# Tiles 2 and 3 of the first block turned in a bank of `psK` instead of `psT`, and another order table for VectorE, ScalarE and the transfers

## The chip, the cores and the metric

The kernel runs on one core of one Trainium2 chip. The metric is the device time of one execution in microseconds (us). Three runs of the kernel before took 1146.65, 1143.88 and 1146.52 us (median 1146.52); one further execution was taken with the hardware profiler.

A core has five engines with queues of their own: TensorE (PE; its weight loads are shown apart as PEld), VectorE (DVE), ScalarE (ACT), GpSimd (POOL) and SyncE (SP), which here issues nearly all transfers. Each runs its instructions in the order in which they were laid down; between engines, semaphores make one wait for another. TensorE writes only to the eight PSUM banks, from which VectorE and ScalarE read.

## The reference, cut to what matters

```python
x = A_x                                    # 2048 x 576
mod = silu(c) @ w_mod                      # six vectors sa, ca, ga, sb, cb, gb
h = layernorm(x) * (1 + ca) + sa
q, k, v = split(h @ wqkv)                  # 32 heads of 18
pq, pk = phi(q), phi(k)                    # phi(t) = where(t > 0, t + 1, exp(t)) + 1e-6
kv, z = sum over s of pk (x) v, sum over s of pk
x = x + ga * ((pq @ kv) / (pq @ z + 1e-6)) @ wo
h = layernorm(x) * (1 + cb) + sb
x = x + gb * (silu(h @ w1) @ w2)           # 576 -> 4608 -> 576
```

## The kernel before

**Stages.** The 2048 tokens are 16 tiles of 128, t = 0 to 15, in four blocks of 512. Every matrix product is done in three passes, with a high and a low half of each factor (`A.copy` makes the high half, `sub_hi` or `w_lo` subtracts it from the full value to get the low one). The first stage, to about 204 us, projects k and v of each tile, sums kv, and projects q of the first half of the tiles. A short stage then builds the product of kv with wo. The second stage, from about 217 us, does the attention of all tiles and the first units of the MLP; the third, from about 370 us to the end, is the MLP alone. TensorE's order is the order of the code throughout.

**The order of the other engines in the first stage.** VectorE, ScalarE, GpSimd and SyncE run the first stage in an order that is written out by hand: the table `FIRST`. `arrange(FIRST, begun)` numbers the instructions of one engine as they stand in the code, and ties each to the one before it in the table. The ties are no waits: they only lay down the queue. So an instruction that the table puts ahead of another is issued first, and whatever stands behind it on that engine waits while it waits.

**The first block.** Its four tiles are read as rows, normalised, and turned: `turn_tiles` lets TensorE transpose 128x128 pieces into PSUM (L452), five per tile, and `modulate` and `split_h` read a piece of two tiles (128x256) from PSUM into `raw`, scale and shift it, and write the high and the low half into `hT` (L213 or L215, L219, L135). Tiles 0 and 1 come first; tiles 2 and 3 are `turn_half`, called behind v(0). Blocks 1 to 3 are turned another way: VectorE transposes 32x32 pieces (L298), a transfer writes them to memory (`turned`, L301) and others read them back (`acc<-turned` L306, `h<-turned` L308); ScalarE and VectorE then modulate and split them (`turn`).

**k, v and q.** k(0) and k(1) are made in passes as the chunks of weights come (L471). Each k and q then goes through phi: ScalarE takes exp from PSUM (e, L373), VectorE takes max(t, 0) + 1e-6 from PSUM (L378) and adds min(e, 1) (L382). A k is split into `pk` (L394 on ScalarE, L135 on VectorE). v goes from PSUM into `vx` in three pieces, each a high half on ScalarE (L643) and a low half on VectorE (L135). v's weights are split by L358 on ScalarE and L363/L365 on VectorE; q's (`wq`) by L358 on ScalarE and L363/L365 on GpSimd. `kv_mm` sums kv (L657). TensorE's order after k(0) and k(1) is: v(0), turn of tiles 2 and 3, v(1), kv of tile 0, q(0), q(1), k(2), v(2), kv, q(2), k(3), and so on.

**PSUM.** The first stage holds three banks for kv (`kvp`; kvp[1] and kvp[2] also serve the turning), one bank `psT`, and two buffers `psK` of two banks each, taken in turn by every `ps2()`: the first turning, k(0), k(1), v(1), q(0), q(1), k(2) and so on, to the five products with wo at L805 (j = 0 to 4). v(0) uses `psT` and kvp[0]. A tile can be written when the tile that had the buffer before has been read out. The second stage has three buffers `big` of two banks and two banks `small` in the same eight banks; the second `big` tile, the one of the first q in this stage, lies in the banks of the first `psK` buffer, and the two `small` ones lie in those of the second.

Of the kernel before, what the change touches and what calls it, by code (L numbers as in the profile page):

```python
# [22 lines left out]
def kernel(ctx: ExitStack, tc, A_x, A_wqkv, A_wo, B_x, B_w1, B_w2, c, w_mod, out):  # L23
# [32 lines left out]
    def behind(instructions):  # L56

        with ExitStack() as order:
# [36 lines left out]

    FIRST = {
        "DVE": """
            2 1 0 4-5 3 6-7 9-10 8 11-13 15 14 16-23 26 24-25 28 27 29-38 43-44 46-47 40 45 48-49 39 41 51 42 50
            53-54 52 55 60 56 61-62 57-58 88-90 63-69 71-72 70 73-75 77-78 76 79-80 91 59 81-87 93 92 94-96 152 97
            99-101 103-104 106-107 98 110-112 102 105 109 113-114 108 127-128 130-131 116 129 132-134 136-137 135  # L100
            138-139 115 119-121 140-146 122 117 123 118 153 124-125 154 147-149 126 155 150-151 156-159 161-162 160
            163-164 193-194 196-197 195 198 165 199-200 202-203 201 204-205 167 171 168 206-211 172-174 212 166 175
            169 176 170 177-184 190-192 185 213-215 186 216-217 219 218 223 220 224 221-222 187 234 238 188 231-232
            189 235-237 233 240-251 225 252-254 230 255-257 239 258-259 226 260 227 261-263 228-229
        """,
        "Activation": """
            0-4 6-7 5 8-10 13 11-12 14-19 21 20 22-25 27-28 26 29 31 30 32 41-43 36 39 33 37 40 48 50 52 38 34 44-47
            49 56 51 57 53 58 35 59 54-55 60-62 65-67 70 73 63 68 64 77 71 78 69 79 75 72 80 76 81-82 74 83 85-87
            91-92 88 84 89-90 93-99 104 101 100 102 107 103 105 111 108 112 106 116-117 109 126-127 113-115 110
            118-125 128-130 133 138 134 131 140 132 139 144 135 141 136 149 137 145 150 142-143 146-148 151-170  # L110
        """,
        "Pool": """
            0-1 3-4 2 6-7 5 8-12 15-17 13-14 18-20
        """,
        "SP": """
            0-30 32-33 31 62 34-38 40-41 39 42-45 48-49 47 46 63-65 50-53 66 54 56-57 55 70-73 58-61 67-68 78-79
            84-88 90-91 89 92-95 80-82 69 74-77 83 96 99 98 100-102 97 106 103-105
        """,
    }

# [100 lines left out]
    def modulate_split(*chunk):  # L221

        modulate(*chunk, A)
        return split_h(*chunk)
# [43 lines left out]
    def psT():  # L268
        t = psA.tile([P, 512], F32, name="psT")
        return t  # L270

    def ps2():
        t = psA.tile([P, 2, 512], F32, name="psK", bufs=2)
        return t
# [174 lines left out]
    def turn_tiles(pT, tiles, chunks):  # L449
        for i in tiles:  # L450
            for k in chunks:
                T.transpose(pT[k][:, i % 2 * P : i % 2 * P + P], x0s[i][:, k * P : (k + 1) * P], ident)  # L452

    def half_args(u, k, pT):
        return pT[k], k, hT[0][:, :, u * 256 : u * 256 + 256], cols["a"], h32[5 * u + k]

    def rooms(t):
        return dict(enumerate((t[:, 0:256], t[:, 256:512], kvp[1][:, 0, :], kvp[1][:, 1, :], kvp[2][:, 0, :])))

    def turn_half():  # L460

        pT = rooms(psT())
        turn_tiles(pT, (2, 3), START)
        for k in START:
            modulate_split(*half_args(1, k, pT))
# [10 lines left out]
    if True:  # L476
# [22 lines left out]
        pT = rooms(ps2()[:, 0, :])  # L499
# [180 lines left out]
    if True:  # L680
        for t in range(NT):
# [18 lines left out]
            if t == 0:  # L700
                for k in START:
                    split_w(wqp_, k, acc[10 + k], G)
                turn_half()
                xx = load_block(1)
# [29 lines left out]
    with tc.manual_schedule(engines={mybir.EngineType.PE}):  # L734
# [57 lines left out]
        rooms = [wg.tile([P, 4 * D], F32, name="w") for _ in range(NP0)]  # L792
# [197 lines left out]
    rooms, rooms0, fp, ts = [], {}, None, None  # L990
# [626 lines left out]
```

## Time and profile before

| | us |
|---|---|
| three runs | 1146.65, 1143.88, 1146.52 |
| the profiled execution, in all | 1145.4 |
| its span, first to last instruction | 1143.7 |
| TensorE busy in the span | 1123.4 |
| VectorE, ScalarE, GpSimd busy | 985.5, 527.2, 658.8 |

The profile is one execution. A page gives busy times and the chain of work that ended last; other views of the same trace give the waits, the groups of instructions, a timeline, and busy times by stretch. Times are in us from the start of the span. A timeline row has the start, the time taken, the engine, the line of the code, the operation, out<-in by the program's names, the shapes, and in brackets the idle time of the engine before it with what ended it. Rows of several instructions (x4) run from the first's start to the last's end; neighbours overlap a little, since an engine begins the next instruction before the last one has left it. "L243" is a line of the code; a helper has one line for all its callers, so the names of the tiles tell more.

The views that matter are shown with the prediction.

### The profile page before, as it was taken

How to read it: one execution, taken by the hardware profiler on the slowest of the kernel's cores; microseconds unless marked ns; L12 is line 12 of the kernel's file. 1: busy time of each engine (PE TensorE's matmuls, PEld its weight loads, DVE VectorE, ACT ScalarE, POOL GpSimd, SP SyncE). 2: the span in 40 equal slices, each digit the busy share in tenths (PEclk: the TensorE clock that was granted, in tenths of full speed). 3: DMA queues.
4: the chain of work that ended last, by engine and by line, in shares of the span. 5: the costliest groups of instructions: out<-in, count | busy, mean ns of one | idle time of the engine just before them, and what ended most of it. 6: DMA issues, size and time to landing. Idle time of an engine off the chain costs nothing.

```text
span 1143.7 us, 19402 instructions
## 1 busy us (share of the span) xinstructions
PE 1123.4 (98%) x7071; PEld 1037.0 (91%) x7071; DVE 985.5 (86%) x1557; ACT 527.2 (46%) x1078; POOL 658.8 (58%) x748
## 2 busy tenths in 40 slices
PE   6999999999999999999999999999999999999998
PEld 4899999899998899999999999999999999999998
DVE  5868765687988999999999999999999999999996
ACT  4644342447455544444445444444454444444441
POOL 3300000454714777767775776677667757776786
PEclk9999999999999999999999999999999999999999
DMA  9367963123458977976968869769779787697684
GB/s 289 81 174 163 168 80 63 56 72 125 151 197 296 369 274 257 343 275 255 362 257 312 312 248 351 273 248 365 263 274 335 263 334 286 253 345 273 250 310 155
DMA packets 103022, 279.03 MB, mean 244 GB/s; under 512 B 40652, under 2 KB 63440, under 8 KB 79888
## 3 DMA queue, kind: packets, MB, share of 16 engines
q1 hardware_dynamic: 102756, 277.50, 70.2%
q8 instruction: 56, 0.92, 0.3%
q10 hardware_dynamic: 172, 0.30, 0.1%
q14 instruction: 38, 0.31, 0.1%
HBM read 256.27 MB, written 21.51 MB: 243 GB/s over the span
## 4 chain that ended last, share of the span: by engine, by line
PE 94%; DMA 3%; DVE 2%; ACT 1%; issue 0%; SPq 0%; DVEq 0%; ACTq 0%
PE up L1348 34%; PE down L1421 32%; PE psK L243 12%; PE big L243 7%; PE small L911 2%; PE big L922 2%; PE kvp L657 2%; DMA acc<-in_A_wqkv_dram 1%; DMA hT<-in_w_mod_dram 1%; PE psK L805 1%; PE big L837 1%; DMA room<-hd 1%; PE small L228 1%; PE up L1451 1%; PE down L1451 1%; DVE st L190 0%
## 5 line engine op out<-in xcount | busy, mean ns | idle before, releaser
L1429 DVE TENSOR_TENSOR acc<-down,acc 128x576 f32<-128x576 f32 x330 | 246.1, 753 | 13.9 <-PE down L1421 4.1
L1348 PE MATMUL up<-hT,w 128*128 128x512 f32 x916 | 240.3, 391 | 0.0
L1348 PEld LDWEIGHTS up<-hT,w 128*128 128x128 f32 x916 | 164.5, 188 | 25.7
L1383 POOL TENSOR_TENSOR s<-f,f 128x256 f32<-128x256 f32 x66 | 51.9, 786 | 163.7 <-ACT f L1364 163.7
L1421 PE MATMUL down<-w,hc 128*128 128x288 f32 x792 | 120.7, 295 | 0.0
L1421 PE MATMUL down<-w,hb 128*128 128x288 f32 x792 | 120.7, 294 | 0.0
L1421 PEld LDWEIGHTS down<-w,hb 128*128 128x128 f32 x792 | 113.6, 188 | 5.9 <-DVE U L1429 0.3
L1421 PEld LDWEIGHTS down<-w,hc 128*128 128x128 f32 x792 | 113.6, 188 | 5.6
L1429 DVE TENSOR_TENSOR U<-down,U 128x576 f32<-128x576 f32 x132 | 99.4, 753 | 18.0 <-PE down L1421 15.7
L135 DVE TENSOR_TENSOR w<-v,w 128x288 fp32r<-128x288 f32 (+1 forms) x170 | 111.6, 666 | 0.1
L243 PE MATMUL psK<-w,hT 128*128 128x256 f32 (+1 forms) x638 | 102.4, 297 | 1.0 <-DVE acc L378 1.0
L1348 PE MATMUL up<-room,w 128*128 128x512 f32 x348 | 93.2, 396 | 1.1 <-DMA room<-hd 1.1
L243 PEld LDWEIGHTS psK<-w,hT 128*128 128x128 f32 x638 | 91.6, 189 | 1.3 <-DVE acc L378 1.3
L1402 POOL TENSOR_TENSOR hc<-s,hc 128x512 fp32r<-128x512 f32 x66 | 89.6, 1358 | 0.0
L1364 ACT ACTIVATE f<-f 128x512 f32<-128x512 f32 x102 | 64.4, 631 | 47.8 <-DVE f L1369 25.4
L1367 DVE TENSOR_TENSOR f<-up,p 128x512 f32<-128x512 f32 x102 | 69.7, 683 | 14.8 <-PE up L1348 10.1
L1348 PEld LDWEIGHTS up<-room,w 128*128 128x128 f32 x348 | 62.4, 188 | 12.4 <-DVE f L1369 1.5
L1091 ACT CAST w<-v 128x288 fp32r<-128x288 f32 x85 | 36.6, 434 | 76.8 <-PE down L1421 54.8
L1387 POOL TENSOR_TENSOR f<-f,s 128x256 f32<-128x256 f32 x66 | 50.9, 771 | 34.3 <-DVE hb L1402 28.7
L196 POOL TENSOR_TENSOR rstd<-ve,neghalf 128x4 f32<-128x4 f32 (+3 forms) x10 | 9.9, 995 | 102.2 <-DVE ve L195 101.2
L1421 PE MATMUL down<-w,hd 128*128 128x288 f32 x396 | 63.3, 295 | 0.0
L1421 PE MATMUL down<-w,he 128*128 128x288 f32 x396 | 63.1, 295 | 0.0
(302 smaller groups left out, 2519.6 us busy)
## 6 DMA issues: line engine op xcount, KB each, us to landing
hT<-hd SPq DMA_DIRECT2D x66, 1280.0 KB, 5.7
hT<-hd SPq DMA_DIRECT2D x45, 1024.0 KB, 4.9
room<-hd SPq DMA_DIRECT2D x35, 1280.0 KB, 6.3
room<-hd SPq DMA_DIRECT2D x20, 1024.0 KB, 5.7
v<-in_B_w_dram SPq DMA_DIRECT2D x17, 576.0 KB, 6.6
v<-in_B_w_dram SPq DMA_DIRECT2D x17, 512.0 KB, 7.5
hd<-S SPq DMA_DIRECT2D x6, 1024.0 KB, 5.9
xt<-in_A_x_dram SPq DMA_DIRECT2D x16, 288.0 KB, 6.0
```

The lines of the kernel that those rows point to most:

```text
L135: return V.tensor_sub(lo, full, f32(hi))
L243: T.matmul(ps, xpart(a), wpart(b), start=n == 0, stop=n == len(XW) - 1)
L657: T.matmul(o, vt[:, j, h, :], pkt[:, :, j * HG : j * HG + P], start=(t == 0 and h == 0 and j % 2 == 0), stop=(t == NT - 1 and h == 1), ski ...
L1091: A.copy(self.w2[n][:, 0], src)
L1348: T.matmul(ps, left, right, start=first and m == 0, stop=m == len(seq) - 1, skip_group_check=True)
L1364: A.activation(self.f[i, k], self.f[i, k], AF.Silu)
L1367: V.tensor_add(f, self.bank[bank[1]], self.p1)
L1383: G.tensor_add(self.s[:, 0:1], half(i, 0, 1), half(i, 1, 1))
L1387: G.tensor_sub(half(i, 1, 0), half(i, 1, 0), self.s[:, 1:2])
L1402: eng.tensor_sub(t[:, :, 1, :], src, f32(t[:, :, 0, :]))
L1421: T.matmul(ps[:, p, :HALF], self.a[i, n][:, u, p * P : (p + 1) * P], self.w.w2[n][:, v], start=n in (1, 5, 7, 6) and j == 0, stop=j == 2, ...
L1429: V.tensor_add(dst, ps[:, :, :HALF], dst)
```

## The change

`turn_half` takes its first bank from `ps2()` instead of `psT()`: chunks 0 and 1 of tiles 2 and 3 are turned in the first bank of a `psK` buffer (the one that k(0) had), chunks 2 to 4 in kvp[1] and kvp[2] as before. One more `psK` tile is taken, so all later ones change their buffer with each other: v(1) takes k(1)'s instead of k(0)'s, and so on to L805.

The table `FIRST` is another one for VectorE, ScalarE and SyncE; GpSimd's is the same, and so are TensorE's order and the number and kind of all instructions. In the new order, among others:

- VectorE: the first four steps of the statistics of tiles 0 and 1 are taken tile by tile, and two of those of tile 2 earlier, among the modulations. max and add of k(0) (L378, L382) come before the last three low halves of v's weights instead of behind them; pk(0) and phi of k(1) come before all of vx(0). Of hT's five low halves of tiles 2 and 3, two stand between the pieces of vx(1), two behind them, and one behind max of q(0).
- ScalarE: one cast of a weight stands before hT's casts. pk(0) and e of k(1) come before the casts of wq; the five modulations come before the first piece of vx(1), and the five casts of hT among and behind its pieces. In blocks 1 to 3 the modulations and casts of hT stand otherwise among the casts of vx, pk and the e of k and q.
- SyncE: two of the four transfers `acc<-turned` of block 2 are issued behind the four loads of xt for block 3, in place of ahead of them; some loads of w_mod are issued later.

```diff
--- before.py
+++ after.py
@@ -95,26 +95,26 @@
 
     FIRST = {
         "DVE": """
-            2 1 0 4-5 3 6-7 9-10 8 11-13 15 14 16-23 26 24-25 28 27 29-38 43-44 46-47 40 45 48-49 39 41 51 42 50
-            53-54 52 55 60 56 61-62 57-58 88-90 63-69 71-72 70 73-75 77-78 76 79-80 91 59 81-87 93 92 94-96 152 97
-            99-101 103-104 106-107 98 110-112 102 105 109 113-114 108 127-128 130-131 116 129 132-134 136-137 135
-            138-139 115 119-121 140-146 122 117 123 118 153 124-125 154 147-149 126 155 150-151 156-159 161-162 160
-            163-164 193-194 196-197 195 198 165 199-200 202-203 201 204-205 167 171 168 206-211 172-174 212 166 175
-            169 176 170 177-184 190-192 185 213-215 186 216-217 219 218 223 220 224 221-222 187 234 238 188 231-232
-            189 235-237 233 240-251 225 252-254 230 255-257 239 258-259 226 260 227 261-263 228-229
+            2 1 0 4-5 3 6-13 15 14 16-23 26 24-25 28 27 29-32 43 33-36 44 37-38 46-47 40 45 48-49 39 41-42 51-52 55
+            50 53-54 56-58 61 60 62 88 63 89 64 90 65-66 68-69 71-72 70 73-75 77-78 76 79-80 91 67 59 81-87 93 92
+            94-96 152 97 99-101 103-104 106-108 98 110-112 102 105 109 113-114 127-128 116 130-131 129 132-134
+            136-137 135 138-139 119-121 115 140-146 122 117 123 118 124-125 153 126 154 147-149 155 150-151 156-159
+            161-162 193-194 163 196-197 195 198-200 202-203 201 204-205 160 165 206-212 168 164 167 171-174 166 175
+            169-170 176-184 190-191 185 192 213-215 219 223 216-217 224 234 218 238 220-222 186-188 231-232 189 233
+            235-237 240-251 225 252-254 230 255-257 239 258-259 226 260 227-228 261-263 229
         """,
         "Activation": """
-            0-4 6-7 5 8-10 13 11-12 14-19 21 20 22-25 27-28 26 29 31 30 32 41-43 36 39 33 37 40 48 50 52 38 34 44-47
-            49 56 51 57 53 58 35 59 54-55 60-62 65-67 70 73 63 68 64 77 71 78 69 79 75 72 80 76 81-82 74 83 85-87
-            91-92 88 84 89-90 93-99 104 101 100 102 107 103 105 111 108 112 106 116-117 109 126-127 113-115 110
-            118-125 128-130 133 138 134 131 140 132 139 144 135 141 136 149 137 145 150 142-143 146-148 151-170
+            0-4 6-7 5 8-10 13 11-12 14-17 21 18-20 22-25 27-28 26 29 31 30 32-34 41-43 39 37 36 48 38 40 50 52 44 46
+            56 45 57 47 49 51 58 53 35 59 54-55 60-62 65-67 70 73-74 63 68 64 77 71 78 69 79 75 72 80 76 81-83 85-87
+            91-92 88 84 89-90 93-98 101-102 99 103-104 100 107 105 111 108 106 116 126-127 112 117 109 113-115 110
+            118-125 128-129 133 130 138 134 140 139 144 141 131 149 145 132 150 135-137 142-143 146-148 151-170
         """,
         "Pool": """
             0-1 3-4 2 6-7 5 8-12 15-17 13-14 18-20
         """,
         "SP": """
-            0-30 32-33 31 62 34-38 40-41 39 42-45 48-49 47 46 63-65 50-53 66 54 56-57 55 70-73 58-61 67-68 78-79
-            84-88 90-91 89 92-95 80-82 69 74-77 83 96 99 98 100-102 97 106 103-105
+            0-30 32 31 33 62 34-38 41 39-40 42-45 47 46 49 48 63-65 50-53 66 54 57 70 72-73 71 55-56 58-61 67-68 78
+            84-87 79 88 91 89-90 92-95 80-81 69 74-77 82-83 96 98-102 97 106 103-105
         """,
     }
 
@@ -459,7 +459,7 @@
 
     def turn_half():
 
-        pT = rooms(psT())
+        pT = rooms(ps2()[:, 0, :])
         turn_tiles(pT, (2, 3), START)
         for k in START:
             modulate_split(*half_args(1, k, pT))
```

## The prediction

> **What bounds the kernel now.** I read the page first.
>
> ```profile
> span 1143.7 us, 19402 instructions
> PE 1123.4 (98%) x7071; PEld 1037.0 (91%) x7071; DVE 985.5 (86%) x1557; ACT 527.2 (46%) x1078; POOL 658.8 (58%) x748
> ...
> PE 94%; DMA 3%; DVE 2%; ACT 1%; issue 0%; SPq 0%; DVEq 0%; ACTq 0%
> ```
>
> TensorE is busy 1123.4 of 1143.7 us, and the chain that ended last is 94% TensorE. No matrix work is added or removed, so the change can only touch the 20.3 us in which TensorE is idle. The next view cuts the span into stretches (us, TensorE busy, weight loads, VectorE, ScalarE, GpSimd, granted clock, DMA share, GB/s) to show where those 20.3 us lie.
>
> ```profile
> 0.00:29.00 29.00, 17.59 (x81) 13.70 (x81) 17.02 (x49) 12.80 (x25) 9.91 (x17) 1.00 0.91 285
> 29.00:56.00 27.00, 25.01 (x186) 24.52 (x187) 23.25 (x48) 17.18 (x36) 10.09 (x7) 1.00 0.31 77
> 56.00:204.00 148.00, 148.00 (x1123) 147.78 (x1121) 100.80 (x177) 58.06 (x114) 4.98 (x7) 1.00 0.68 127
> 204.00:220.00 16.00, 14.65 (x78) 12.11 (x77) 9.60 (x15) 7.53 (x13) 7.82 (x8) 1.00 0.25 78
> 220.00:1143.00 923.00, 918.11 (x5610) 838.87 (x5608) 834.80 (x1271) 431.62 (x892) 626.01 (x710) 1.00 0.73 269
> ```
>
> 11.4 us lie before 29 us, where input transfers set the pace; 2.0 between 29 and 56; none from 56 to 204, although the table reorders that stretch too; 1.35 from 204 to 220; 4.9 in the 923 us after. Third, the waits of TensorE from 29 to 220 us (waiter, releaser, us, times, longest):
>
> ```profile
> PE psK L243 <- DVE acc L378: 1.0, 1, 1.0
> PE big L243 <- DVE v L365: 1.0, 1, 1.0
> PE psT L452 <- DVE vx L135: 0.9, 1, 0.9
> ```
>
> Three long waits, 1.04 + 0.98 + 0.93 = 2.95 of the 3.35 us that the two stretches lack: that is nearly all there is to win between 29 and 220 us. I then went to each in the timeline, which has the exact figures.
>
> ```profile
> 33.41 0.28 PE L243 MATMUL psT<-w,hT 128*128 128x256 f32 x1
> ...
> 35.58 0.44 PE L452 MATMUL psT<-ident,xt 128*128 128x128 f32 x2 [0.93 <-DVE vx L135]
> ...
> 41.71 7.63 PE L243 MATMUL psK<-wq,hT 128*128 128x288 f32 x56
> 49.18 0.48 PE L243 MATMUL psK<-w,hT 128*128 128x288 f32 x2
> ...
> 54.15 0.54 PE L243 MATMUL psK<-w,hT 128*128 128x256 f32 x2 [1.04 <-DVE acc L378]
> ...
> 217.29 0.71 PE L837 MATMUL big<-ident,w 128*128 128x128 f32 x5
> 218.98 3.20 PE L243 MATMUL big<-wq,hT 128*128 128x288 f32 x22 [0.98 <-DVE v L365]
> ```
>
> 35.58 is the turning of tiles 2 and 3, which waits until v(0) is read out of the same bank. 41.71 is q(0) and q(1), 49.18 is k(2), 54.15 is v(2), which waits until q(1) has left its bank. 218.98 is the first q with the later pool `big`.
>
> **The change, part by part.** VectorE, ScalarE and GpSimd around these places:
>
> ```profile
> 29.64 1.43 DVE L363 TENSOR_TENSOR w<-acc,w 128x576 fp32r<-128x576 f32 x2
> 30.99 0.75 DVE L363 TENSOR_TENSOR w<-acc,v 128x576 fp32r<-128x576 f32 x1
> 32.56 0.76 DVE L378 TENSOR_SCALAR a<-psK 128x576 f32<-128x576 f32 x1
> 33.35 1.84 DVE L382 SCALAR_TENSOR_TENSOR a<-e,a 128x576 f32<-128x576 f32 x1
> 35.12 0.41 DVE L135 TENSOR_TENSOR vx<-psT,vx 128x252 fp32r<-128x252 f32 x1
> ...
> 42.93 0.23 DVE L135 TENSOR_TENSOR vx<-psK,vx 128x72 fp32r<-128x72 f32 x1 [0.28 <-ACT vx L643]
> 43.08 1.75 DVE L135 TENSOR_TENSOR hT<-raw,hT 128x256 fp32r<-128x256 f32 x5
> ...
> 53.38 0.72 DVE L378 TENSOR_SCALAR acc<-psK 128x576 f32<-128x576 f32 x1
> ```
>
> ```profile
> 29.68 0.65 ACT L373 ACTIVATE e<-psK 128x576 f32<-128x576 f32 x1
> ...
> 32.40 1.81 ACT L358 CAST wq<-acc 128x576 fp32r<-128x576 f32 x3
> ...
> 35.38 0.67 ACT L394 CAST pk<-a 128x576 fp32r<-128x576 f32 x1
> ...
> 40.35 0.71 ACT L219 CAST hT<-raw 128x256 fp32r<-128x256 f32 x2
> ```
>
> ```profile
> 38.45 3.40 POOL L363 TENSOR_TENSOR wq<-acc,wq 128x576 fp32r<-128x576 f32 x2
> ```
>
> *The bank of the turned tiles.* The ten transposes stay as they are; four of them now write a `psK` bank, whose k(0) VectorE reads out long before. The 0.93 us wait at 35.58 goes. Its cover is the early read of k(0) (L378): if that came after about 34.6, the wait would be back.
>
> *phi of k(0) ahead of three splits of w.* VectorE now runs L378 and L382 before the last three low halves of v's weights (the second of 29.64, 30.99, and the half one of L365 behind it). L378 follows e (29.68 + 0.65 = 30.33, in the new order about 0.45 earlier, since one weight cast moved ahead): about 29.9. L382 starts 0.79 later and holds VectorE 1.77, so the splits start near 32.45 and, 0.67 apart (two take 1.43, one 0.76), end at 33.2, 33.9 and 34.55. v(0) wants them from 33.41 on, 0.27 apart, and starts about 0.3 earlier than now (VectorE's last split of hT moves up by 0.5, and the wait for it, 0.25 at 29.01, goes; the row stands with the last rival): it waits step by step, ends near 35.1 instead of 34.5, and then transposes at once. Gain and loss meet: v(1) starts 0 to 0.35 us earlier. I take 0.2, the middle; it turns out to be covered by the next step.
>
> *pk(0) and e of k(1) ahead of the casts of wq on ScalarE.* pk waits for L382 (ends 32.55), and pk and e take a slot of 0.57 and 0.55 (0.67 and 0.65 less the overlap of 0.1 that the three casts in 1.81 show): the casts of wq start near 33.7 instead of 32.40. GpSimd's five low halves hang on them and run without pause to 38.45 + 3.40 = 41.85; now to about 43.15. The last one is chunk 1, which q(0) needs from its fifth pass, eight issues of 0.133 (7.48 us for 56) after 41.71, so at 42.77. Today it is there 0.9 early; after the change TensorE gets to this pass at 43.15 + 0.05 (the delay seen at 54.15 behind 53.38 + 0.72) = 43.2, +0.43 us, whatever v(1) gained. The bounds are 0.1 (GpSimd catching up on the way) and 0.9 (the casts another 0.5 late); I keep 0.43.
>
> *hT's low halves among the vx.* Two of the five 0.35 us steps of the row at 43.08 go into the pauses ahead of vx (0.28 in the row above, larger ones before it), one goes behind q(0)'s L378 but still ahead of q(1)'s, and v(1)'s first vx comes some 0.5 earlier, because ScalarE's casts of hT no longer stand before it (two of them take 0.71). From 42.93 to 53.38 VectorE has no pause, so q(1)'s L378 comes 0.5 + 0.35 = 0.85 earlier: it ends at 53.25.
>
> *v(2), the first sum.* TensorE ends k(2) 28 issues of 0.134 behind 49.18, near 52.93, and 0.43 later in the new order: 53.36, just behind VectorE's 53.25 + 0.05. So v(2) starts at 53.36 instead of 54.15: -0.8 us. The bounds are -0.3 (q(0) waiting 0.9) and -0.85 (VectorE alone decides).
>
> *Parity of the banks.* `psK` has two buffers in turn. One tile more is taken in the first block, so from there on each `psK` tile lies in the other buffer. That matters once, at 218.98: this `big` tile reuses the banks of one of them, and today that is the last one used (j = 4 at L805); now it is the one before (j = 3).
>
> ```profile
> 217.19 0.76 DVE L363 TENSOR_TENSOR v<-psK,w 128x576 fp32r<-128x576 f32 x1 [1.19 <-ACT w L358]
> 218.16 0.76 DVE L365 TENSOR_TENSOR v<-psK,v 64x576 fp32r<-64x576 f32 x1 [0.21 <-ACT v L358]
> ```
>
> j = 3 is read out at 217.95, when TensorE is still at L837 until 218.00. The 0.98 us wait shrinks to at most 0.1: -0.9 us, bounds -0.75 and -0.98. The buffer of j = 4 goes to `small`, which the first q don't use.
>
> *All else in the table* (the order of work on the later blocks, and of transfers) lies where TensorE never waits now. I cost it at 0; its cover is the distance of a k, v or q from the release of its bank. Upper bound: see the first rival.
>
> Sum: -0.8 - 0.9 = **-1.7 us**, bounds 1.05 and 1.85 below. Behind 220 us everything hangs on TensorE and moves with it. The profiled execution took 1145.4 us in all, 1143.7 of it span, which gives 1143.7. The runs shown are 1143.88, 1146.52 and 1146.65; the middle of all four is 1145.95, and 1145.95 - 1.7 = **1144.25 us** is the forecast.
>
> **The rivals.**
>
> *Slower: the second block comes back late.* Sync's queue now puts two of the four transfers `acc<-turned` of the second block behind four loads of xt. The rows of 96 to 106 us (KB each, median us to landing), one later transfer, and ScalarE's first use:
>
> ```profile
> xt<-in_A_x_dram SPq DMA_DIRECT2D x4, 288.0 KB, 8.8
> acc<-turned SPq DMA_DIRECT2D x4, 256.0 KB, 7.0
> ```
>
> ```profile
> raw<-parts SPq DMA_DIRECT2D x1, 576.0 KB, 13.2
> ```
>
> ```profile
> 107.12 1.52 ACT L213 ACTIVATE acc<-acc,col_a 128x512 f32<-128x512 f32 x2
> ```
>
> Issued near 99.3, at 7.0 or 8.8 they land at 106.3 or 108.1; ScalarE wants them from about 106.5. With 13.2 they land at 112.5, and ScalarE stands 5.4 us with the readouts of q and k behind it. Two buffers of 3.7 us each, less a readout of 0.65 + 0.76, give TensorE about 2 us of grace: it stalls 3.4, net +1.7, **1147.65**. It decides from a landing of about 10 us on. For it: this stretch already has the fullest DMA engines. Against it: VectorE's use of that block for k(8), at 125 us, leaves many us, and 13.2 belongs to a transfer of far smaller pieces.
>
> *No gain: the lead is handed back.* The longest wait of TensorE behind 220 us is for a transfer:
>
> ```profile
> PE up L1348 <- DMA room<-hd: 1.1, 1, 1.1
> ```
>
> Were that transfer paced by the queue instead of by TensorE, the 1.7 would end there: **1145.95**. Against it: the DMA engines are 73% busy there, and what is stored is computed from TensorE's own results.
>
> *Faster: the new waits don't appear.* If GpSimd and the splits keep up, all three waits go in full: -2.95, **1143.0**. Against it: GpSimd's five steps have no pause to catch up in, and the splits stand behind 0.76 + 1.84 us of work by order.
>
> *The slow start lasts longer.* The profile grants the full clock in every stretch, yet the early matmuls are slower:
>
> ```profile
> 15.98 1.78 PE L471 MATMUL psK<-w,hT 128*128 128x288 f32 x6 [1.15 <-DVE raw L215]
> ...
> 29.01 1.86 PE L471 MATMUL psK<-w,hT 128*128 128x288 f32 x12 [0.25 <-DVE hT L135]
> ```
>
> Six there take 1.78 us, twelve of the same shape here 1.86: 0.24 against 0.13 each. If the 24 that follow 24.8 us ran like the first, they would add 24 x 0.11 = 2.6: **1146.85**. Against it: nothing before 22 us moves. The Trainium skill (TensorE: Matmul & The Clock Gate, Part 1: The HAM clock gate) says that the array runs at half rate until a free-running window of about 3.4 us has been busy, and that the point of change varies from run to run. The doubled spacing agrees with it, the granted clock of 1.00 does not; by that rule the time could lie up to half a window, an estimated 1.7 us, to either side with no change at all.
>
> **How the numbers follow.** The forecast has 0.58, the faster case 0.13, no gain 0.15, the late block 0.09, the slow start 0.05. 1144.25 is the likeliest case's. Its own bounds are 1144.1 to 1144.9; the three runs shown lie 2.8 us (0.24%) apart, so 0.3%, 3.4 us, is about what a measurement of this kernel can tell from no change. The range 1142.0 to 1147.2 takes in the faster case and no gain with that spread and leaves out most of the late block. Faster by over 0.3% (below 1142.5): nearly half of the faster case and a sixth of the forecast, 0.16. Slower by over 0.3%: the worse third of the late block and of the slow start, a tenth of no gain, and a little for what I don't see: 0.08. The rest, 0.76, is within 0.3%.
>
> **What would show it.** Right: no wait at the transposes of tiles 2 and 3; small waits of v(0) on L363 and L365; one of 0.3 to 0.9 us of q(0) on GpSimd; none at v(2); at the second `big` 0.1 or less; TensorE full from 56 to 204 us; the 923 us after 220 unchanged to 1 us. Wrong: any TensorE wait between 56 and 204, above all on ScalarE near 107 us; a wait at `big` as long as now; or a changed length of the stretch after 220.

## The result, and the profile after

| | before | after |
|---|---|---|
| median of 22 runs each, us | 1145.63 | 1143.63 |
| span from lowest to highest, us | 1143.88 to 1147.1 | 1142.26 to 1147.72 |
| profiled execution in all, its span, us | 1145.4, 1143.7 | 1142.27, 1140.6 |

The ratio of the runs is 0.9987 with a 95% interval of 0.9981 to 0.9993: 1.5 us faster, 0.8 to 2.2 (the medians lie 2.0 apart). That is within 0.3%, and the interval leaves out 1. The page of the kernel after (span; busy time of each engine; shares of the chain that ended last):

```profile
span 1140.6 us, 19406 instructions
PE 1122.1 (98%) x7071; PEld 1036.0 (91%) x7071; DVE 985.2 (86%) x1557; ACT 526.9 (46%) x1078; POOL 659.6 (58%) x748
...
PE 96%; DVE 2%; DMA 1%; ACT 0%; issue 0%; ACTq 0%; DVEq 0%; SPq 0%
```

The work is the same, and the chain is TensorE's still more. The same cut by stretch as before (us, busy time of TensorE, weight loads, VectorE, ScalarE, GpSimd, then granted clock, DMA share, GB/s):

```profile
0.00:29.00 29.00, 17.37 (x88) 13.93 (x89) 18.00 (x50) 13.81 (x27) 10.48 (x17) 1.00 0.95 285
29.00:56.00 27.00, 26.07 (x194) 25.34 (x193) 23.87 (x49) 16.70 (x35) 9.03 (x6) 1.00 0.36 90
56.00:204.00 148.00, 147.63 (x1114) 146.81 (x1113) 99.33 (x175) 59.04 (x117) 5.76 (x8) 1.00 0.67 125
204.00:220.00 16.00, 16.00 (x95) 14.01 (x94) 10.58 (x17) 5.69 (x10) 8.60 (x9) 1.00 0.26 79
```

Idle time between 29 and 56 us fell from 1.99 to 0.93, between 204 and 220 from 1.35 to nothing. The 0.37 us that 56 to 204 now lacks are an old wait at the first L805, which has moved from 204.72 to 202.87 and so into this stretch. The waits of TensorE from 29 to 220 us (waiter, releaser, us, times, longest), then the rows of its timeline at the places of the prediction:

```profile
PE psK L243 <- POOL wq L363: 0.5, 1, 0.5
PE psK L805 <- ACT acc L375: 0.4, 1, 0.4
PE psK L243 <- DVE acc L378: 0.3, 1, 0.3
```

```profile
29.70 0.28 PE L243 MATMUL psT<-w,hT 128*128 128x256 f32 x1
...
33.17 0.35 PE L243 MATMUL psT<-w,hT 128*128 128x256 f32 x1
...
33.79 0.38 PE L452 MATMUL psK<-ident,xt 128*128 128x128 f32 x2
...
34.80 0.52 PE L243 MATMUL psK<-w,hT 128*128 128x256 f32 x2
...
41.66 6.66 PE L243 MATMUL psK<-wq,hT 128*128 128x288 f32 x48 [0.50 <-POOL wq L363]
...
52.36 0.54 PE L243 MATMUL psK<-w,hT 128*128 128x256 f32 x2 [0.32 <-DVE acc L378]
...
215.44 0.71 PE L837 MATMUL big<-ident,w 128*128 128x128 f32 x5
216.16 4.00 PE L243 MATMUL big<-wq,hT 128*128 128x288 f32 x28
```

29.70 is the start of v(0), 33.17 the pass of v(0) that waits a little for a split, 33.79 the turning of tiles 2 and 3 with no wait, 34.80 v(1), 41.66 q(0) waiting for GpSimd, 52.36 v(2), 216.16 the second `big` tile with no wait.

The steps behind v(0) are told as differences from its start, since that start itself varies from one execution to the next (30.71 before, 29.70 here; more on this at the end). The same three steps, for every kernel of this study (us; each number is a start in that kernel's timeline of TensorE or the difference of two, "q of big" being the first q in a `big` tile; in three kernels, marked *, v(2) starts within a row of six passes, and its start is reckoned from the spacing):

| kernel | v(0) | v(2) - v(0) | q of big - v(2) | ratio to before, 95% |
|---|---|---|---|---|
| before | 30.71 | 23.44 | 164.83 | |
| after | 29.70 | 22.66 | 163.80 | 0.9987 (0.9981, 0.9993) |
| after, once more | 29.52 | 22.65 | 163.84 | 0.9986 (0.9977, 0.9994) |
| bank alone | 30.25 | 27.87 | 163.78 | 1.0038 (1.0026, 1.0051) |
| table alone | 30.02 | 26.30 | 164.75 | 1.0034 (1.0020, 1.0047) |
| parity back | 32.34 | 22.55 | 164.38 | 0.9993 (0.9984, 1.0002) |
| q in order | 30.03 | 22.83 | 163.83 | 0.9984 (0.9975, 0.9992) |
| both waits * | 31.44 | 21.38 | 164.36 | 0.9983 (0.9974, 0.9992) |
| phi late | 30.32 | 23.93 | 163.98 | 0.9990 (0.9981, 0.9999) |
| hT behind | 30.18 | 22.70 | 163.79 | 0.9985 (0.9976, 0.9994) |
| pk behind | 30.13 | 22.20 | 163.90 | 0.9977 (0.9967, 0.9986) |
| max between * | 31.82 | 21.37 | 165.02 | 0.9980 (0.9971, 0.9989) |
| pk behind, z moved | 30.05 | 22.25 | 164.18 | 0.9983 (0.9973, 0.9992) |
| max between, z moved * | 30.01 | 22.18 | 164.33 | 0.9985 (0.9977, 0.9994) |

The change took 0.78 us from the way v(0) to v(2) and 1.03 from v(2) to the first q in `big`: 1.81 us from v(0) on. The runs, at 1.5 (0.8 to 2.2), agree with it.

A part of v(0)'s earlier start is the change's too. Ahead of v(0) the last passes of k(0) and k(1) waited twice for VectorE in the kernel before (28.26 below, and 29.01 in the prediction), and no longer do; the second row is of the kernel after:

```profile
28.26 0.50 PE L471 MATMUL psK<-w,hT 128*128 128x288 f32 x2 [0.24 <-DVE w L365]
```

```profile
27.00 2.86 PE L471 MATMUL psK<-w,hT 128*128 128x288 f32 x20
```

From VectorE's first copy of `e` (L438, at 22.86 before and 22.28 after) to v(0) it is 7.85 us before and 7.86 with the bank alone. With the new table it is 7.40 to 7.42 in the nine profiles whose clock was not cut there. So the table takes 0.44 us ahead of v(0), and the steps of the profiles come to 2.25 us, a little above the interval of the runs.

### The profile page after: what moved, and what is told of

It is laid out like the page before. It is cut to its first block, busy times and chain, and to the rows that moved or that the text cites. A ratio compares the mean times of both kernels' runs of the same rounds, so it can differ in the third digit from the quotient of the medians.

```text
span 1140.6 us, 19406 instructions
## 1 busy us (share of the span) xinstructions
PE 1122.1 (98%) x7071; PEld 1036.0 (91%) x7071; DVE 985.2 (86%) x1557; ACT 526.9 (46%) x1078; POOL 659.6 (58%) x748
## 4 chain that ended last, share of the span: by engine, by line
PE 96%; DVE 2%; DMA 1%; ACT 0%; issue 0%; ACTq 0%; DVEq 0%; SPq 0%
PE up L1348 34%; PE down L1421 32%; PE psK L243 12%; PE big L243 7%; PE small L911 2%; PE big L922 2%; PE kvp L657 2%; PE psK L805 1%; PE big L837 1%; PE psK L471 1%; DMA room<-hd 1%; PE small L228 1%; PE up L1451 1%; PE down L1451 1%; DMA tmod<-in_w_mod_dram 1%; DVE hT L135 0%
## 5 line engine op out<-in xcount | busy, mean ns | idle before, releaser
L1348 PE MATMUL up<-hT,w 128*128 128x512 f32 x916 | 240.4, 391 | 0.0
L1348 PEld LDWEIGHTS up<-hT,w 128*128 128x128 f32 x916 | 164.5, 188 | 25.9
L1348 PE MATMUL up<-room,w 128*128 128x512 f32 x348 | 93.2, 396 | 1.1 <-DMA room<-hd 1.1
L1348 PEld LDWEIGHTS up<-room,w 128*128 128x128 f32 x348 | 62.4, 188 | 12.3 <-DVE f L1369 1.5
L196 POOL TENSOR_TENSOR rstd<-ve,neghalf 128x4 f32<-128x4 f32 (+3 forms) x10 | 9.8, 976 | 98.4 <-DVE ve L195 67.5
```

Of the source, the lines that this page charges most:

```text
L1348: T.matmul(ps, left, right, start=first and m == 0, stop=m == len(seq) - 1, skip_group_check=True)
```

## The experiments

**The changed kernel once more.**

> The changed kernel once more, for a second profile and a second timing. Theory (the gain is three waits between 29 and 220 us: 0.93 at the transposes of tiles 2 and 3, 1.04 at v(2) less what is left of it, 0.98 at the second big tile): the waits of TensorE from 29 to 220 us are again 0.5 on GpSimd, 0.3 at v(2) and none at big, and the time is 1.5 to 2 us below the kernel before. Rival (much of the 3.1 us between the two profiled spans is the early stretch, which comes out by chance): the start of v(0), 29.70 us in the changed kernel and 30.7 in the one before, comes anywhere between the two, and the span moves with it.

1143.13 us against 1144.98 for the kernel before, ratio 0.9986. The three waits are the same to 0.1 us, and so are both differences in the table. Yet the span of this execution is 1143.1, 2.5 us longer than that of the first. v(0) came earlier, not later: the rival is wrong about the place. The excess lies at one later wait:

```profile
377.12 1.93 PE L1348 MATMUL up<-room,w 128*128 128x512 f32 x6 [2.33 <-DMA room<-hd]
...
381.14 1.81 PE L1348 MATMUL up<-hT,w 128*128 128x512 f32 x6
...
378.00:382.00 4.00, 4.00 (x15) 3.42 (x14) 2.06 (x3) 1.49 (x3) 3.83 (x6) 0.57 0.68 234
```

The first two rows are its timeline, the third a stretch of 4 us there. The same rows in the first execution of this kernel:

```profile
375.98 1.65 PE L1348 MATMUL up<-room,w 128*128 128x512 f32 x6 [1.07 <-DMA room<-hd]
...
378.72 1.53 PE L1348 MATMUL up<-hT,w 128*128 128x512 f32 x6
```

TensorE waited 2.33 us for the transfer `room<-hd` instead of 1.07, and behind it TensorE was granted 0.57 of its clock over 4 us, which cost 1.3 us more: the lag behind the first execution is 377.12 - 375.98 = 1.14 at the wait and 381.14 - 378.72 = 2.42 a little on. A difference of a single pair of spans is therefore no measure of this change. Each run has its granted clock on record. In this batch the runs at 1.000 average 1142.75 us (7 of 11) against 1144.86 for the kernel before (18 of 21): 2.1 us, near the 2.25 of the steps. So cut clocks may be what brings the ratio down to 1.6 us, but this rests on few runs.

**Bank and table, each alone.**

The kernel before with the bank of the kernel after:

```diff
-        pT = rooms(psT())
+        pT = rooms(ps2()[:, 0, :])
```

The kernel after with the bank of the kernel before:

```diff
-        pT = rooms(ps2()[:, 0, :])
+        pT = rooms(psT())
```

> The bank of the turned tiles is changed, the order table is the old one. Theory (bank and table are one edit: v(1) now takes k(1)'s buffer, and the old table reads k(1) late, e at 38.28 and L378 at 38.99 + 0.76 us): the 0.93 us wait at the transposes goes and the 0.98 at big goes, but v(1) waits until about 39.8 us, some 3 us later than its 36.65; net 2 us slower than the kernel before, about 1147.7. Rival (the parts add up, each removes its own wait): 0.93 at the transposes is swallowed by v(2), 0.98 at big stays won, 1.0 us faster than before, about 1144.6.

> The new order table, but tiles 2 and 3 are turned in psT as before. Theory (bank and table are one edit): the transposes wait for the low half of vx out of psT, which the new table puts behind phi of k(1), at 35.98 + 0.40 us instead of 33.79: a wait of about 2.6 us, of which the 0.5 on GpSimd is given back; the 1.0 at big is there again; net 3 us slower than the changed kernel, about 1 to 1.5 us slower than the kernel before. Rival (the parts add up): the table's 0.8 us at v(2) is kept, and it is 0.8 to 1 us faster than the kernel before.

Both are slower than the kernel before, by 4.3 and 3.9 us by their ratios. So the parts don't add up; each needs the other. The rows of the bank alone, its timeline and then two stretches (the number before the last two is the granted clock):

```profile
39.36 0.51 PE L243 MATMUL psK<-w,hT 128*128 128x256 f32 x2 [4.12 <-DVE a L378]
39.70 0.43 PE L243 MATMUL psK<-v,hT 128*128 128x256 f32 x2
39.98 3.24 PE L243 MATMUL psK<-w,hT 128*128 128x256 f32 x14
...
40.00:42.00 2.00, 2.00 (x11) 2.00 (x11) 0.00 (x1) 0.52 (x2) 1.28 (x1) 0.60 1.06 227
42.00:44.00 2.00, 2.00 (x10) 2.00 (x10) 0.00 (x0) 0.00 (x0) 0.00 (x0) 0.55 0.63 226
```

v(1) now lies in k(1)'s buffer, and the old table reads k(1) late: a wait of 4.12 us at just the time expected. And of the table alone:

```profile
36.85 0.41 PE L452 MATMUL psT<-ident,xt 128*128 128x128 f32 x2 [2.56 <-DVE vx L135]
...
38.00:40.00 2.00, 2.00 (x10) 2.00 (x9) 0.23 (x1) 1.58 (x4) 1.92 (x2) 0.50 0.21 30
```

The wait for the low half of vx, 2.56 us, is the 2.6 that theory named. What no theory named is the rest: behind both waits TensorE ran at half its clock for about 3.4 us, which costs an estimated 1.7 us, half of that. The fourteen passes of v(1) that take 2.05 us in the kernel after took 3.24 with the bank alone. That is most of the 2.3 us (bank alone) and 2.4 to 2.9 us (table alone) by which they came out slower than expected. The table of differences also shows the two edits apart where they don't meet: with the new bank the way from v(2) to `big` is 163.8, with the old one 164.8, whatever the table.

**The parity of the banks, undone in the changed kernel.**

```diff
-        psz = ps2()
+        psz = psT(), kvp[0].rearrange("p a b -> p (a b)")
...
-        A.copy(halves(z), psz[:, :, :HALF])
+        for h in range(2):
+            A.copy(z[:, h * HALF : (h + 1) * HALF], psz[h][:, :HALF])
```

(ScalarE's later table is numbered anew for the second copy.)

> The changed kernel, with the product for z in psT and kvp[0] instead of a psK tile, read out in two copies: one psK tile less, so the last five tiles change buffers again. Theory (the second big tile waits for whichever product with wo had its banks last): the wait of about 1.0 us at big is back; the 0.37 us wait at the first L805 goes, since this tile no longer has the buffer of the q just ahead; net +0.6 us on the changed kernel. Rival (the wait at big went because VectorE is earlier there, not because of the bank): big doesn't wait, net -0.4 us on the changed kernel.

The ratio is 0.9993 against 0.9986 for the changed kernel in the same batch, +0.8 us where +0.6 was expected (the intervals overlap; the profile is what decides here). Its timeline, whose line numbers are 5 lower:

```profile
205.11 2.10 PE L801 MATMUL psK<-raw,tmod 126*128 126x288 f32 x8
...
217.58 0.71 PE L833 MATMUL big<-ident,w 128*128 128x128 f32 x5
219.27 0.93 PE L238 MATMUL big<-wq,hT 128*128 128x288 f32 x5 [0.98 <-DVE v L360]
```

The wait at `big` is back with its old length, on the same split of the last product, and the 0.37 us wait at the first product (205.11) is gone. VectorE's order is that of the changed kernel, so the bank is the cause. As the programs are built, the second `big` tile lies in PSUM banks 4 and 5 before, after and here; the last product (j = 4) lies in 4 and 5 before and here, and in 6 and 7 in the changed kernel.

**q's weights in the order of use.** The changed kernel casts and splits chunks 2, 3, 4 of `wq` before 0 and 1. Here it goes 0 to 4 (the casts on ScalarE, the low halves on GpSimd).

```diff
-            ... 32-34 41-43 39 37 36 48 38 40 50 52 ...
+            ... 32-34 39-42 37 36 48 38 43 50 52 ...
-            0-1 3-4 2 6-7 5 8-12 15-17 13-14 18-20
+            0-1 3-4 2 6-7 5 8-20
```

> The changed kernel with the weights of q cast and split in the order in which q(0) uses them (chunks 0 and 1 first in place of last). Theory (the waits of q(0) and v(2) are in series: TensorE's and VectorE's ways to v(2) are 0.32 us apart): the 0.50 us wait on GpSimd goes, v(2) waits 0.8 instead of 0.3, the time stays that of the changed kernel to 0.2 us. Rival (a wait that is removed is won): 0.5 us faster than the changed kernel.

Ratio 0.9984 beside 0.9986 and 0.9987, and the wait moved on, as expected:

```profile
40.19 7.63 PE L243 MATMUL psK<-wq,hT 128*128 128x288 f32 x56
...
52.86 0.53 PE L243 MATMUL psK<-w,hT 128*128 128x256 f32 x2 [1.31 <-DVE acc L378]
```

q(0) and q(1) run through; v(2) waits 1.31 instead of 0.32, more than the 0.8 expected, and starts 22.83 us behind v(0), no earlier than without the edit. VectorE's max of q(1) is what v(2) stands on.

**Both waits taken away.**

```diff
-            ... 91 67 59 81-87 93 92 94-96 ...
+            ... 91 67 59 81-85 93 86-87 92 94-96 ...
```

(q's weights are in the order of use here too.)

> As the one before, and on VectorE max of q(1) stands behind two of block 1's four transposes instead of all four, 1.37 us earlier. Theory (in series): now both waits go, 0.5 + 0.3 = 0.8 us faster than the changed kernel, about 2.3 to 2.8 below the kernel before, and TensorE has no wait from 34 to 202 us. Rival (two transposes come 0.7 us later, block 1 comes back later and another wait takes the place): a new wait between 56 and 204 us, no gain.

v(2) comes 1.28 us earlier against v(0) than in the changed kernel, without a wait; but on the way to `big` 0.56 is given back, and the ratio, 0.9983, can't be told from the changed kernel's. The rows, of TensorE (at 52.19 four passes of k(2) and the first two of v(2) stand in one row) and of ScalarE:

```profile
52.19 1.18 PE L243 MATMUL psK<-w,hT 128*128 128x288 f32 x6
...
77.45 1.35 PE L243 MATMUL psK<-w,hT 128*128 128x288 f32 x6
```

```profile
69.57 1.52 ACT L213 ACTIVATE acc<-acc,col_a 128x512 f32<-128x512 f32 x2 [0.99 <-DMA acc<-turned]
```

ScalarE waits 0.99 us for block 1 to come back through memory, and reads out the tiles behind it late. Six passes at 77.45 take 1.35 us where they take 0.96 in the changed kernel: TensorE stands there in pieces too small for the list of waits. The rival was right that another wait takes the place; which step hands ScalarE's delay on to these six passes the trace doesn't say.

**phi of k(0) behind the splits again.**

```diff
-            ... 39 41-42 51-52 55 50 53-54 56-58 ...
+            ... 39 41-42 51 50 53-54 52 55-58 ...
```

> The changed kernel with phi of k(0) on VectorE (L378, L382) behind the last three splits of v's weights again. Theory (phi of k(0) is early for the sake of pk(0), e of k(1) and the casts of wq behind them on ScalarE, not of the bank): v(0) doesn't wait (0.3 us won), the transposes don't either, but pk(0) comes 1.4 us later, GpSimd ends 1.4 later and q(0) waits 1.6 to 1.9 us instead of 0.5; v(2)'s 0.3 goes; together 0.8 to 1.1 us slower than the changed kernel. Rival (the splits and phi may stand either way): no more than 0.3 us either way.

v(2) came 1.27 us later against v(0) than in the changed kernel, where 0.8 to 1.1 was expected; by the ratios, 0.9990 against 0.9985 to 0.9987, it is some 0.5 us, and the intervals overlap. So the direction was right by the steps, the size is open, and the places were not all foreseen:

```profile
36.11 0.54 PE L243 MATMUL psK<-w,hT 128*128 128x256 f32 x2 [0.76 <-DVE a L378]
...
41.99 1.07 PE L243 MATMUL psK<-wq,hT 128*128 128x288 f32 x6 [0.38 <-POOL wq L363]
43.56 6.67 PE L243 MATMUL psK<-wq,hT 128*128 128x288 f32 x48 [0.50 <-POOL wq L363]
```

0.76 us of it is v(1) at 36.11, waiting for max of k(1), whose buffer it has. q(0) waits 0.88 in two pieces instead of 0.50, not the 1.6 to 1.9 expected, and the 0.3 at v(2) stays. So the early phi of k(0) serves both GpSimd and the reading out of k(1).

**hT's low halves behind vx(1).**

```diff
-            ... 62 88 63 89 64 90 65-66 68-69 ... 91 67 59 81-87 ...
+            ... 62 88-90 63-69 ... 91 59 81-87 ...
```

> The changed kernel with all five low halves of hT on VectorE behind the three pieces of vx(1) and ahead of q(0)'s max, as in the old table. Theory (the two low halves that fill VectorE's pauses, and the one behind q(0)'s max, bring q(1)'s max forward): q(1)'s max ends 0.7 us later, v(2) waits 1.0 instead of 0.3, 0.7 us slower than the changed kernel. Rival (VectorE has the time anyway, and only the order of ScalarE and the earlier v(1) count): v(2) waits 0.3 as now, no difference.

Nothing was lost: v(2) starts 22.70 us behind v(0) (22.66), and the ratio is 0.9985. The waits shifted a little (0.32 at q(0) instead of 0.50, 0.51 at v(2) instead of 0.32), with the same sum. Theory falls; the rival holds on the time, not on the wait at v(2) as such. VectorE's rows here:

```profile
41.81 1.76 DVE L135 TENSOR_TENSOR hT<-raw,hT 128x256 fp32r<-128x256 f32 x5
...
52.11 0.72 DVE L378 TENSOR_SCALAR acc<-psK 128x576 f32<-128x576 f32 x1
```

In the changed kernel max of q(1) starts at 51.59, with v(0) 0.48 us earlier: 21.89 behind v(0) there, 21.93 here. The low halves that were put in VectorE's pauses took part of those pauses waiting for ScalarE's casts, it seems, and won no more than the one behind q(0)'s max cost.

**Towards a faster kernel.** Four more, each built on the order of use of `wq`: pk(1)'s low half behind the add of q(0) ("pk behind"); with that, max of q(1) between two pairs of transposes ("max between"); and each of these two with the product for z moved as in the experiment on parity, and one `big` buffer taken and not used, so that q would get another one.

```diff
-            ... 91 67 59 81-87 93 92 94-96 ...
+            ... 91 67 81-87 93 92 59 94-96 ...
```

"max between":

```diff
-            ... 91 67 81-87 93 92 59 94-96 ...
+            ... 91 67 81-85 93 86-87 92 59 94-96 ...
```

The unused buffer, in the last kernel:

```diff
+    skip = [big]
     def late_q():
+        if skip:
+            skip.pop()()
         q_proj(next(qs), big, pb)
```

> The changed kernel with q's weights split in the order of use, and on VectorE the low half of pk(1) behind max of q(1) and add of q(0) in place of ahead of block 1's transposes, which all come 0.67 us earlier. Theory (the waits of q(0) and v(2) are in series, and block 1's way back by ScalarE limits what follows): both waits go, no stretch behind them gets later, 0.8 us faster than the changed kernel, ratio to the kernel before about 0.998. Rival (block 1 comes back by transfers that start no earlier): v(2) doesn't wait but k(4) or v(3) does, 0.3 us faster at most.

> As the one before, with the product for z in psT and kvp[0], and with one big buffer skipped, so that the second big tile lies in the banks that kvp[2] and psT had. Theory (each wait there comes from one bank): neither the 0.37 us wait at the first L805 nor one at big, 0.37 us faster than the one before; TensorE has no wait over 0.3 us from 29 to 350 us; ratio about 0.9975. Rival (the readout of z in two copies puts ScalarE late for the products behind it): a new wait at L805 or at the first q of the next stage, no gain.

> q's weights split in the order of use, the low half of pk(1) behind add of q(0) (as in the run before last), and max of q(1) again between the second and the third of block 1's transposes. Theory (q(0) and v(2) in series, and block 1's way back has less than 1 us to spare): the wait of 0.7 at v(2) goes, and since the last transpose is no later than in the changed kernel, at most 0.3 of it comes back between 68 and 80 us: about 0.8 us faster than the changed kernel, ratio to the kernel before 0.9975 to 0.998. Rival (what is won ahead of block 1 is always given back behind it): as in the run with both waits taken away, 0.5 us given back, ratio 0.9983.

> As the one before, with the product for z in psT and kvp[0], and with one big buffer skipped just ahead of the first q of the second stage (in the earlier run it was skipped one tile too late), so that this q lies in the banks of kvp[2] and psT. Theory (each of these waits comes from one bank): neither the 0.37 us wait at the first L805 nor the 1.0 at big, 0.37 us faster than the one before, TensorE busy all 16 us from 204 to 220. Rival (the two copies of z put ScalarE late): a new wait takes the place of one of them, no gain.

"pk behind" has the best ratio of all, 0.9977 (0.9967 to 0.9986), but v(2) starts just 0.46 us earlier against v(0) than in the changed kernel and still waits 0.70, and the intervals overlap: that it beats the changed kernel isn't shown. "max between" takes 1.29 us off the way to v(2) and gives 1.22 back on the way to `big`; ratio 0.9980, so again nothing that can be told from the changed kernel. Its rows, of TensorE and ScalarE:

```profile
75.22 0.50 PE L243 MATMUL psK<-w,hT 128*128 128x288 f32 x2 [0.78 <-DVE vx L135]
```

```profile
70.61 1.52 ACT L213 ACTIVATE acc<-acc,col_a 128x512 f32<-128x512 f32 x2 [1.84 <-DMA xt<-in_A_x_dram]
```

ScalarE's L213 reads the rows of block 1 that come back through memory, and again it is late. The row names a load of `xt`, but those loads were issued from 67.5 us on and took 5.9 us, so they can't have released ScalarE at 70.61; block 1's own transfers, ahead of them in SyncE's queue, are likelier.

The two kernels with z moved had ratios of 0.9983 and 0.9985. In both the 0.37 us wait at the first product is gone, and in both the 0.98 at `big` is back, against the expectation. This does not speak against the bank: as these programs are built, the unused tile takes up no buffer, and q still lies in banks 4 and 5, those of j = 4. So this way round the bank was not found.

The last of them has the order of "max between" up to the product for z, and shows how far one profile can be trusted. Its rows, of TensorE and VectorE:

```profile
48.38 0.53 PE L238 MATMUL psK<-w,hT 128*128 128x288 f32 x2 [0.58 <-DVE acc L373]
```

```profile
44.00 1.54 DVE L185 BATCH_NORM_STATS2 st<-xt 128x6 f32<-128x288 f32 x4 [1.23 <-DMA xt<-in_A_x_dram]
```

VectorE waited 1.23 us for block 1's load, where it waited 0.51 in "max between" and not at all in the changed kernel; max of q(0) came later, k(2) waited 0.58 us for it, and v(2) came 0.48 us earlier against v(0) than in the changed kernel, not 1.29. Two profiles of one order thus differ by 0.8 us in this step, and the landing of that load is what differs ahead of it. A kernel without any of the waits between 29 and 220 us was not reached.

## Why the prediction was right, and where it wasn't

The forecast was -1.7 us; the ratio gives -1.5, the way from v(0) to `big` -1.81, and with the 0.44 ahead of v(0) -2.25. The forecast counts from the start of the span and has v(0) 0.3 earlier in it, so its steps have to be set against differences that take in those 0.44. By its own steps:

**The wait at the transposes** went, as said: 33.79 follows without a pause.

**The three splits.** The term that was mis-sized is phi of k(0). I took the add (L382) at 1.77 us from its row of 1.84; moved, it took 0.76. VectorE's rows of the kernel after:

```profile
29.35 0.76 DVE L378 TENSOR_SCALAR a<-psK 128x576 f32<-128x576 f32 x1
30.14 0.76 DVE L382 SCALAR_TENSOR_TENSOR a<-e,a 128x576 f32<-128x576 f32 x1
...
32.27 0.76 DVE L365 TENSOR_TENSOR w<-acc,w 64x576 fp32r<-64x576 f32 x1
```

And the group of this operation in the kernel before (count, then shortest, median and longest in ns):

```profile
L382 DVE SCALAR_TENSOR_TENSOR a<-e,a x16: 737/757/1845, 33.4 to 191.3; 128x576 f32<-128x576 f32 x16
```

The splits end at 33.03, 3.33 us behind v(0)'s start; by the forecast it was 4.1 (34.55, with v(0) at 30.4). v(0) waits once, 0.27 us (33.17 against 32.63 + 2 x 0.135), and v(1) starts 0.84 us earlier against v(0) (5.10 us behind it, 5.94 before). With the 0.44 ahead of v(0) that is 1.28 us, where the forecast had 0.2. 1.84 was the longest of sixteen; the median of 0.757 would have been the better price.

**q(0) behind GpSimd**: forecast 0.43, measured 0.50. But both sides of it came 1.5 us earlier than I had them, GpSimd's last low half at 38.61 + 3.00 = 41.61 instead of 43.15, since pk(0) follows the same add, and v(0) started 1.01 earlier in this profile. The row of GpSimd:

```profile
38.61 3.00 POOL L363 TENSOR_TENSOR wq<-acc,wq 128x576 fp32r<-128x576 f32 x2
```

**Max of q(1)** came 0.78 us earlier against v(0) (53.38 - 30.71 = 22.67 before, 21.89 after), 1.22 with what lies ahead of v(0), and I had said 0.85. My reason was wrong: I gave it to hT's low halves among vx and an earlier first vx. hT's place makes 0.04 us, as its experiment shows. VectorE follows v(1), which came 0.84 earlier against v(0).

**v(2)**: -0.78 from v(0) on, -1.22 with the 0.44 ahead of it. The forecast was -0.8 with bounds of -0.3 and -0.85, so this term was sized too small. I had TensorE and VectorE ready for v(2) at almost the same time, and no wait; v(2) still waits 0.32, so VectorE alone sets its start. That -0.78 looks like -0.8 is chance, and so is part of the closeness of -1.7 to the -1.5 of the runs.

**Parity**: the full 0.98 went where I kept 0.9, and the experiment on parity shows the cause; the rows of the table with the old bank and the new one (164.8 and 163.8 from v(2) to `big`, with either table) agree.

**The rest at 0**: no wait of TensorE is listed from 56 to 202 us. The lead of 2.82 us at `big` (of which 1.01 is v(0)'s start) is 3.28 at L1348 and 3.1 at the end.

Of the rivals, *the late second block* was near. ScalarE did wait for that block, by its last transfers (`h<-turned`), and TensorE didn't:

```profile
108.56 0.82 ACT L213 ACTIVATE acc<-acc,col_a 128x512 f32<-128x512 f32 x1 [1.21 <-DMA h<-turned]
```

Its 2 us of grace are right for one buffer (3.7 less 0.65 + 0.76 is 2.3), not for the two that the working names.

*No gain*: the wait at L1348 is not paced by the queue in a way that eats the lead, 1.07 us after and 1.14 before, but it scatters between 0.79 and 2.33 over the profiles. *New waits don't appear*: they did. *The slow start*: see below; it is real, and profiles with one and the same order show it and don't. "Nothing before 22 us moves" was not so: the first statistics of tiles 0 and 1, at 3.9 to 5.9 us, did move. What I did not see is how little is left behind the waits: with q(0)'s and v(2)'s gone, 0.56 of 1.28 us came back as new waits in one kernel and 1.22 of 1.29 in another. In both, ScalarE waited for block 1 in front of them, so block 1's way through memory is the likely next limit; but both profiles had a late start by a cut clock as well, and no experiment moved block 1 alone. The 2.95 us of the list of waits were not all to be had by reordering VectorE.

## What to carry to other kernels

A list of waits is not a list of gains: waits in a row share one slack, and removing one (0.50 us at q(0)) only moved it to the next. Where a bank and an order table change together, cost them together, since each alone was 4 us slower here. And take a price from the group's median, not from the one row that stands at the place.

## What the hardware showed beside that

**A late TensorE pays twice.** Behind waits of 4.12, 2.56 and 2.33 us the granted clock fell to between 0.50 and 0.60 for about 3.4 us, and that cost another 1.2 us or more (3.24 - 2.05 in the fourteen passes above); behind one of 2.12 (at L1348 with the bank alone) it stayed at 1.00, as behind all shorter ones from 29 us on. The drop begins 0.6 to 1.2 us after TensorE has resumed. The Trainium skill (TensorE: Matmul & The Clock Gate, Part 1: The HAM clock gate) gives half rate after an idle window of about 3.4 us, and windows that run free of the kernel. The half rate and its length agree; a gap of 2.33 us was enough here, which is shorter than that window.

**The start scatters by itself.** In the profiles v(0) starts between 29.52 and 32.34 us. In three of them the clock was cut for 3.4 us from between 25 and 26.1 us on, though no wait of TensorE since 14 us was longer than 1.15, and v(0) starts at 31.44 or later; without a cut it starts at 30.71 at the latest. Here is 26 to 29 us in the kernel with parity back, and in the changed kernel:

```profile
26.00:29.00 3.00, 3.00 (x13) 2.90 (x14) 2.90 (x10) 2.89 (x6) 0.00 (x0) 0.52 0.74 223
```

```profile
26.00:29.00 3.00, 3.00 (x24) 2.98 (x23) 2.90 (x8) 3.00 (x6) 0.82 (x1) 1.00 0.90 262
```

Thirteen matmuls against twenty-four in the same 3 us, at 0.52 and 1.00, with the same order on every engine up to there. These 2 us, and the wait at L1348 with the cut behind it, are as large as the whole effect of the change; they can account for runs of one kernel that lie 3 to 5 us apart. The granted clocks on record fit: of the 22 runs of the changed kernel, the twelve at 1.000 average 1143.1 us, the three at 0.998 or less 1146.8.

**The slow add.** L382 took 1.84 us at 33.35 in the kernel before, right behind the start of GpSimd's splits at 33.14, 1.54 in the kernel with phi late, where GpSimd starts 0.5 us before it, and 0.76 where GpSimd hasn't begun (30.14 in the kernel after, whose next one, at 34.72 beside GpSimd, took 1.01). The Trainium skill (GPSIMD Engine Reference, 1. Specifications) says that GpSimd shares its interface to SBUF with VectorE's instructions that have two SBUF inputs, which this is. But the next such add of the kernel before took 0.76 with GpSimd at work from 38.45 on, so that alone doesn't decide it, and what does stays open:

```profile
39.79 0.76 DVE L382 SCALAR_TENSOR_TENSOR a<-e,a 128x576 f32<-128x576 f32 x1
```
